# Moving columns taken alternately from the two halves of the operand, in the float32r matmuls of a spectral layer with two MLPs

## The chip, the cores and the metric

The kernel runs on one core of a Trainium2 chip. The metric is the device time in microseconds (us) of one execution. Engines: PE (TensorE) with its weight loads (PEld), DVE (VectorE), ACT (ScalarE), POOL (GpSimd), SP (the queue that issues most DMAs).

## The reference, cut to what matters

```
X = rfft(x, axis=1)                      # x: 2 x 3008 x 256, float32
Yr = Xr @ w_r - Xi @ w_i + b_r           # the mixing, 256 x 256
Yi = Xr @ w_i + Xi @ w_r + b_i
Y  = soft-threshold(Yr, 0.01) + 1j * soft-threshold(Yi, 0.01)
y  = irfft(Y, n=3008, axis=1)            # -> 6016 tokens x 256
h  = y @ w_in;  g = max(h, 0) + alpha * min(h, 0);  z = g @ w_out      # 256 -> 2048 -> 256
h  = z @ w_in2; g = where(h >= 1, h, where(h <= -1, 0, (h + 1)**2 / 4));  out = g @ w_out2
```

## The kernel before, in words

The transform of length 3008 = 47 x 64 is done in two stages. `f1` multiplies by a 47-point matrix (float32, 256 columns), stores its result to DRAM (`store_a`, halves 0 and 1 of the frequencies), and `load_a` brings it back in another layout. Then come 24 items (2 batches x 12), in the loop over `j`: `f2(j+2)` (the second forward matrices, tiles `m_t[0..2]`, eight frequencies each, so four items each), `mix(j)` (the mixing), `i1(j-2)` (the first inverse matrices, `n_t[0..2]`); `p3` is the second inverse stage and writes `y`. From item 16 on `p3` and the conversion of the first MLP's weights lie beside the items.

Where more than single-pass precision is wanted, an operand is split into a high and a low part of type float32r (`split`: the high part by ACT or DVE, the low part by DVE), and three matmuls are added up: low x high, high x low, high x high. `mm3` does this for the MLPs (L95 to L97), `mix` does it by itself (L324 to L326). In the MLPs the moving operand is the activation, 512 tokens (a chunk; the sixth chunk of each batch has 448), and the stationary operand is a block of 128 x 128 weights. In `mix` the moving operand is the weight `wm`, 256 columns, and the stationary one is the data. `f1`, `f2`, `i1` and `p3` use float32 operands without a split; each such matmul is two records in the trace.

An MLP step (layer l, chunk c, hidden block f) has two parts: `first` computes 128 hidden units of the chunk (6 matmuls into `psh`), the activation function and the split into `gh`, `gl`; `second`, three steps later, adds their share to the two output blocks `pso` (6 matmuls). After the last f the output is copied from `pso` to `y` (L439) and, in the second layer, stored. `prep` splits the next chunk's input into `mxh`, `mxl`. There are 2 x 12 x 16 = 384 steps. All tokens of a chunk are independent columns, so their order inside a chunk may be any, as long as the copy at the end puts them back.

The order on each engine is the program's order, written out by hand. So is that of SP's DMAs, which it issues one after the other; one that has to wait holds up all that follow:

```
    load_mn(0, n_t, c_i1)          # L282
    for g in range(8):
        store_a(g, 1)
    load_mn(1, m_t, c_f2)          # L285
    load_a(0, A_PARTS[3:])
    load_mn(2, m_t, c_f2)
    for g in range(8, 16):
        f1(g)
        store_a(g, 0)
    load_mn(1, n_t, c_i1)
```

Of the kernel before, what the change touches and what calls it, by code (L numbers as in the profile page):

```python
# [9 lines left out]
F32R = mybir.dt.float32r  # L10
U32 = mybir.dt.uint32
AF = mybir.ActivationFunctionType
# [9 lines left out]
NF = DFF // 128  # L22
# [53 lines left out]
def spectral_mlp_kernel(ctx: ExitStack, tc: tile.TileContext, x, w_r, w_i, bias, c_f1, c_f2,  # L76
                        c_i1, c_i2, w_in1, w_out1, alpha, w_in2, w_out2, out):
    nc = tc.nc
    V, A, G, T = nc.vector, nc.scalar, nc.gpsimd, nc.tensor

    base = ctx.enter_context(tc.tile_pool(name="base", bufs=1))
    rot = ctx.enter_context(tc.tile_pool(name="rot", bufs=2))
# [3 lines left out]
    def split(src, hi, lo, hi_engine):  # L86

        if hi_engine is A:
            A.activation(hi, src, AF.Copy)  # L89
        else:  # L90
            V.tensor_copy(hi, src)  # L91
        V.tensor_tensor(lo, src, hi.bitcast(F32), op=ALU.subtract)  # L92

    def mm3(ps, wh, wl, xh, xl, start, stop):
        T.matmul(ps, wl, xh, start=start, stop=False)  # L95
        T.matmul(ps, wh, xl, start=False, stop=False)  # L96
        T.matmul(ps, wh, xh, start=False, stop=stop)  # L97
# [5 lines left out]
    def block(tag, shape, dtype, name):  # L103
        return base.tile(shape, dtype, tag=tag, name=name)
# [22 lines left out]
    def w_of(l, k, f, h, sl):  # L127
        return wt[l, f][:, h, 256 * k + sl * 128:256 * k + sl * 128 + 128]
# [76 lines left out]
    ps = psum.tile([128, 256], F32, tag="h", name="ps_warm")  # L205
# [20 lines left out]
    def load_a(b, parts):  # L226
        if a_sb[b] is None:
            a_sb[b] = block(f"a{b}", [128, NK, D], F32, f"a_{b}")
        for k, n in parts:
            h, k0 = divmod(k, NK // 2)  # L230
            src = a_dr[b][h].rearrange("t (q k) f -> (t q) k f", q=4)
            nc.sync.dma_start(a_sb[b][:, k:k + n, :], src[:, k0:k0 + n, :])

    def store_a(g, h):
        b, j = divmod(g, 8)
        nc.sync.dma_start(a_dr[b][h][4 * j:4 * j + 4].rearrange("t p f -> p t f"), aes[g][48 * h:48 * h + 48])

    def load_mn(k, tiles, src):
        nc.sync.dma_start(tiles[k].rearrange("p k f -> p (k f)"), src[:, 1024 * k:1024 * (k + 1)])

    a_sb, aes = [None] * B, {}

# [21 lines left out]
    m_t = [block(f"m{k}", [128, 8, 128], F32, f"m{k}") for k in range(3)]  # L264
    n_t = [block(f"m{3 + k}", [128, 8, 128], F32, f"n{k}") for k in range(3)]
    wm32 = [rot.tile([128, 2, D], F32, tag="tb", name=f"wm32_{k}") for k in range(2)]
# [3 lines left out]
    for g in range(8):  # L270
        f1(g)
        store_a(g, 0)
        load_x(8 + g)
        if g == 3:
            nc.sync.dma_start(m_t[0][:, 0:4, :].rearrange("p k f -> p (k f)"), c_f2[:, 0:512])
    nc.sync.dma_start(wm32[0], w_r.rearrange("(c p) e -> p c e", p=128))
    load_a(0, A_PARTS[:2])
    nc.sync.dma_start(wm32[1], w_i.rearrange("(c p) e -> p c e", p=128))
    nc.sync.dma_start(m_t[0][:, 4:8, :].rearrange("p k f -> p (k f)"), c_f2[:, 512:1024])
    load_a(0, A_PARTS[2:3])  # L280
    nc.sync.dma_start(b_t[:, 0, :], bias)
    load_mn(0, n_t, c_i1)  # L282
    for g in range(8):
        store_a(g, 1)
    load_mn(1, m_t, c_f2)  # L285
    load_a(0, A_PARTS[3:])
    load_mn(2, m_t, c_f2)
    for g in range(8, 16):
        f1(g)
        store_a(g, 0)  # L290
    load_mn(1, n_t, c_i1)
    wm = [block(f"c{k}", [128, 2, 2, D], F32R, f"wm{k}") for k in range(2)]
    for k in range(2):
        split(wm32[k], wm[k][:, 0], wm[k][:, 1], A)


    items = [(b, i) for b in range(B) for i in range(NK // 2)]
# [17 lines left out]
    def mix(b, i):  # L315
        xh, xl = xt.pop((b, i))
        ps = psum.tile([128, 2, D], F32, tag="o", name=f"psm{b}_{i}")
        for k in range(2):
            o = ps[:, k, :]
            for c in range(2):  # L320
                j = 2 * k + c
                for r, off in ((0, 64), (1, 0)):
                    last = c == 1 and r == 1
                    T.matmul(o, xl[:, j, off:off + 128], wm[r][:, 0, c, :], start=c == r == 0, stop=False)  # L324
                    T.matmul(o, xh[:, j, off:off + 128], wm[r][:, 1, c, :], start=False, stop=False)  # L325
                    T.matmul(o, xh[:, j, off:off + 128], wm[r][:, 0, c, :], start=False, stop=last)  # L326
        cl_ = rot.tile([128, 2, D], F32, tag="ta", name=f"clip{b}_{i}")
        t = rot.tile([128, 2, D], F32, tag="tb", name=f"t{b}_{i}")
        y32 = rot.tile([128, 2, D], F32, tag="gh", bufs=4, name=f"y32_{b}_{i}")
        V.tensor_tensor(t, ps, b_t.to_broadcast([128, 2, D]), op=ALU.add)  # L330
        V.tensor_scalar(cl_, t, LAM, -LAM, op0=ALU.min, op1=ALU.max)
        V.tensor_tensor(y32, t, cl_, op=ALU.subtract)
        y_32[b, i] = y32
# [14 lines left out]
    chunks = []  # L348
    for b in range(B):
        c0 = 0  # L350
# [3 lines left out]
    NMAX = max(CHUNKS)  # L354
    NC = len(chunks)
    xc, gt, po = {}, {}, {}

    def window(n):

        return slice(0, n) if n == NMAX else slice(16, 16 + n)  # L360

    def prep(l, c):
        b, c0, n = chunks[c]

        tags = ("p1", "p2") if (l, c) == (0, 0) else (f"c{2 * (c % 2)}", f"c{2 * (c % 2) + 1}")
        xh, xl = (block(t, [128, 2, NMAX], F32R, f"mx{h}{l}_{c}")[:, :, window(n)] for t, h in zip(tags, "hl"))
        split(y[b][:, :, c0:c0 + n], xh, xl, A)
        xc[l, c] = xh, xl

    vs, y = {}, [None] * B  # L370

# [16 lines left out]
    def late_split(step):  # L388
        return step[0] == 1 or step[1] < 2 or step[1] == NC - 1

    def split_late(step):
        if step is not None and late_split(step):
            gh, gl, ta = gt[step]
            split(ta, gh, gl, A)

    def first(l, c, f, before):
        n = chunks[c][2]
        xh, xl = xc[l, c]
        ps = psum.tile([128, NMAX], F32, tag="h", name=f"psh{l}_{c}_{f}")[:, :n]
        for d in range(2):  # L400
            mm3(ps, w_of(l, 0, f, 0, d), w_of(l, 0, f, 1, d), xh[:, d, :], xl[:, d, :], d == 0, d == 1)
        gh = rot.tile([128, NMAX], F32R, tag="gh", bufs=4, name=f"gh{l}_{c}_{f}")[:, window(n)]
        gl = rot.tile([128, NMAX], F32R, tag="gl", bufs=4, name=f"gl{l}_{c}_{f}")[:, window(n)]
        ta = rot.tile([128, NMAX], F32, tag="ta", name=f"ta{l}_{c}_{f}")[:, :n]
        tb = rot.tile([128, NMAX], F32, tag="tb", name=f"tb{l}_{c}_{f}")[:, :n]
        gt[l, c, f] = gh, gl, ta
        if l == 0:

            A.activation(ta, ps, AF.Relu, scale=-1.0)  # L409
            A.activation(tb, ps, AF.Relu)  # L410
            split_late(before)
            V.scalar_tensor_tensor(ta, ta, nalpha[:, f:f + 1], tb, op0=ALU.mult, op1=ALU.add)  # L412
            if not late_split((l, c, f)):
                split(ta, gh, gl, V)
        else:

            A.activation(ta, ps, AF.Relu, bias=0.5, scale=0.5)  # L417
            V.scalar_tensor_tensor(tb, ta, 1.0, ta, op0=ALU.min, op1=ALU.mult)  # L418
            split_late(before)
            V.tensor_tensor(ta, ps, tb, op=ALU.max)  # L420

    def second(l, c, f):
        b, c0, n = chunks[c]
        gh, gl, _ = gt.pop((l, c, f))
        if f == 0:
            po[l, c] = [psum.tile([128, NMAX], F32, tag="o", name=f"pso{e}_{l}_{c}")[:, :n] for e in range(2)]
        for e in range(2):
            mm3(po[l, c][e], w_of(l, 1, f, 0, e), w_of(l, 1, f, 1, e), gh, gl, f == 0, f == NF - 1)
        if f == NF - 1:
            for e in range(2):  # L430
                dst = y[b][:, e, c0:c0 + n]
                if e and (l, c) == (1, NC - 1):
                    k = n // 2
                    V.tensor_copy(dst[:, :k], po[l, c][e][:, :k])
                    A.activation(dst[:, k:], po[l, c][e][:, k:], AF.Copy)
                    A.dma_start(out[:, e, b * S + c0 + k:b * S + c0 + n], dst[:, k:])
                    nc.sync.dma_start(out[:, e, b * S + c0:b * S + c0 + k], dst[:, :k])
                    continue
                A.activation(dst, po[l, c][e], AF.Copy)  # L439
                if l == 1:  # L440
                    nc.sync.dma_start(out[:, e, b * S + c0:b * S + c0 + n], dst)

    conv = conversions(0, list(range(NF)), V, V)
    n = len(items)
# [3 lines left out]
    for j in range(n):  # L448
        if j + 2 < n:
            f2(*items[j + 2])  # L450
        mix(*items[j])
        if j >= 2:
            i1(*items[j - 2])
# [22 lines left out]
        if j == n - 2:  # L476
            prep(0, 0)
# [13 lines left out]
    for i in range(len(seq) + DEPTH):  # L491
        if i < len(seq):
            l, c, f = seq[i]
# [57 lines left out]
```

## Time and profile before

| | us |
|---|---|
| median of 3 runs | 1208.13 (1204.58 to 1208.75) |
| the profiled execution, its own time | 1207.99 |
| its span | 1206.2 |
| PE busy / PEld / DVE / ACT / POOL | 1198.1 / 1025.4 / 905.7 / 607.4 / 80.4 |
| granted TensorE clock, mean | 0.999 |

A matmul's record begins before it streams and ends when its last result is modelled to be out, so two records that follow each other overlap; what a matmul costs is read from the distance between the starts of records, not from their length. Column order in the rows of a timeline: start in us, length in us, engine, line, operation, output <- inputs, shape, number of records merged, and in brackets the idle time before and what ended it.

### The profile page before, as it was taken

What the parts mean: (1) busy time and instruction counts of PE and PEld (TensorE: products, weight loads), DVE (VectorE), ACT (ScalarE), POOL (GpSimd) and SP (SyncE); (2) the same over time, 40 slices, a digit from 0 to 9 for tenths busy, and PEclk for the clock granted to TensorE, in tenths of its full rate; (3) what the DMA queues carried; (4) which work ended last, traced back from release to release, by engine and by line L of the source; (5) the groups of instructions that cost most, each with busy time, mean ns of one, the idle gap of its engine ahead of it and who ended that gap; (6) DMA issues with size and microseconds to landing.
All of it is one profiled execution on the core that took longest, in us unless ns stands there. A gap on an engine that the chain in (4) does not pass through costs nothing.

```text
span 1206.2 us, 15623 instructions
## 1 busy us (share of the span) xinstructions
PE 1198.1 (99%) x5862; PEld 1025.4 (85%) x5862; DVE 905.7 (75%) x1409; ACT 607.4 (50%) x1131; POOL 80.4 (7%) x64
## 2 busy tenths in 40 slices
PE   9999999999999999999999999999999999999998
PEld 6899988888888988888888988888889888888888
DVE  3489977368889999888875676777777777777775
ACT  3455676565555555554444644444444444444443
POOL 0000000001213131231200000000000000000000
PEclk9999999999999999999999999999999999999999
DMA  9995660010100101000000000000000000000000
GB/s 280 311 306 170 189 187 15 1 35 18 36 18 18 35 19 36 18 30 6 1 1 18 1 1 18 18 1 18 18 1 18 17 1 18 18 18 1 18 18 16
DMA packets 37180, 59.30 MB, mean 49 GB/s; under 512 B 3248, under 2 KB 25200, under 8 KB 37104
## 3 DMA queue, kind: packets, MB, share of 16 engines
q1 hardware_dynamic: 23536, 41.37, 10.7%
q10 hardware_dynamic: 13568, 16.93, 4.5%
q8 instruction: 46, 0.75, 0.3%
q14 instruction: 30, 0.25, 0.1%
HBM read 39.55 MB, written 18.74 MB: 48 GB/s over the span
## 4 chain that ended last, share of the span: by engine, by line
PE 96%; DMA 3%; SPq 1%; issue 0%; ACT 0%; DVE 0%
PE pso L97 14%; PE psh L97 14%; PE pso L96 14%; PE psh L96 14%; PE pso L95 14%; PE psh L95 14%; PE ps L383 2%; PE psm L324 2%; PE psm L325 2%; PE psm L326 2%; PE psi L339 2%; PE psf L304 2%; DMA x<-in_x 1%; DMA n<-in_c_i 1%; DMA a_dr<-ae 1%; DMA m<-in_c_f 0%
## 5 line engine op out<-in xcount | busy, mean ns | idle before, releaser
L92 DVE TENSOR_TENSOR gl<-ta,gh 128x512 fp32r<-128x512 f32 (+1 forms) x384 | 274.7, 715 | 60.8 <-ACT gh L89 55.8
L95 PE MATMUL pso<-gh,w 128*128 128x512 f32 (+1 forms) x768 | 296.0, 385 | 0.0
L95 PE MATMUL psh<-mxh,w 128*128 128x512 f32 (+1 forms) x768 | 295.8, 385 | 0.0
L96 PE MATMUL pso<-gl,w 128*128 128x512 f32 (+1 forms) x768 | 295.6, 385 | 0.0
L97 PE MATMUL pso<-gh,w 128*128 128x512 f32 (+1 forms) x768 | 295.5, 385 | 0.0
L96 PE MATMUL psh<-mxl,w 128*128 128x512 f32 (+1 forms) x768 | 295.5, 385 | 0.0
L97 PE MATMUL psh<-mxh,w 128*128 128x512 f32 (+1 forms) x768 | 295.5, 385 | 0.0
L417 ACT ACTIVATE ta<-psh 128x512 f32<-128x512 f32 (+1 forms) x192 | 113.1, 589 | 279.1 <-PE psh L97 279.1
L418 DVE SCALAR_TENSOR_TENSOR tb<-ta 128x512 f32<-128x512 f32 (+1 forms) x192 | 130.7, 681 | 143.4 <-ACT ta L417 143.4
L409 ACT ACTIVATE ta<-psh 128x512 f32<-128x512 f32 (+1 forms) x192 | 113.3, 590 | 235.2 <-PE psh L97 190.0
L412 DVE SCALAR_TENSOR_TENSOR ta<-ta,nalpha,tb 128x512 f32<-128x512 f32 (+1 forms) x192 | 166.9, 869 | 30.0 <-ACT tb L410 29.4
L96 PEld LDWEIGHTS psh<-mxl,w 128*128 128x128 f32 x768 | 144.2, 188 | 27.2
L96 PEld LDWEIGHTS pso<-gl,w 128*128 128x128 f32 x768 | 144.2, 188 | 26.9 <-DVE gl L92 0.2
L95 PEld LDWEIGHTS psh<-mxh,w 128*128 128x128 f32 x768 | 144.0, 188 | 27.0
L95 PEld LDWEIGHTS pso<-gh,w 128*128 128x128 f32 x768 | 144.1, 188 | 26.5
L97 PEld LDWEIGHTS psh<-mxh,w 128*128 128x128 f32 x768 | 144.2, 188 | 26.3
L97 PEld LDWEIGHTS pso<-gh,w 128*128 128x128 f32 x768 | 144.1, 188 | 26.2
L89 ACT ACTIVATE gh<-ta 128x512 fp32r<-128x512 f32 (+1 forms) x240 | 147.6, 615 | 1.3 <-DVE ta L420 1.3
L420 DVE TENSOR_TENSOR ta<-psh,tb 128x512 f32<-128x512 f32 (+1 forms) x192 | 129.2, 673 | 0.0
L410 ACT ACTIVATE tb<-psh 128x512 f32<-128x512 f32 (+1 forms) x192 | 112.3, 585 | 0.0
L91 DVE CAST gh<-ta 128x512 fp32r<-128x512 f32 (+1 forms) x144 | 68.1, 473 | 15.2 <-PE pso L97 0.5
L324 PE MATMUL psm<-wm,fl 128*128 128x256 f32 x192 | 56.3, 293 | 0.2 <-DVE fl L311 0.2
(56 smaller groups left out, 889.2 us busy)
## 6 DMA issues: line engine op xcount, KB each, us to landing
u<-in_w_in ACTq DMA_DIRECT2D x32, 256.0 KB, 2.7
u<-in_w_out ACTq DMA_DIRECT2D x32, 256.0 KB, 3.0
v_dr<-ve SPq DMA_DIRECT2D x12, 512.0 KB, 3.0
v<-v_dr SPq DMA_DIRECT2D x16, 384.0 KB, 5.1
x<-in_x SPq DMA_DIRECT2D x15, 384.0 KB, 7.5
out<-yt SPq DMA_DIRECT2D x20, 256.0 KB, 2.1
a<-a_dr SPq DMA_DIRECT2D x6, 768.0 KB, 7.5
a_dr<-ae SPq DMA_DIRECT2D x20, 192.0 KB, 7.0
```

The lines of the kernel that those rows point to most:

```text
L89: A.activation(hi, src, AF.Copy)
L92: V.tensor_tensor(lo, src, hi.bitcast(F32), op=ALU.subtract)
L95: T.matmul(ps, wl, xh, start=start, stop=False)
L96: T.matmul(ps, wh, xl, start=False, stop=False)
L97: T.matmul(ps, wh, xh, start=False, stop=stop)
L324: T.matmul(o, xl[:, j, off:off + 128], wm[r][:, 0, c, :], start=c == r == 0, stop=False)
L409: A.activation(ta, ps, AF.Relu, scale=-1.0)
L410: A.activation(tb, ps, AF.Relu)
L412: V.scalar_tensor_tensor(ta, ta, nalpha[:, f:f + 1], tb, op0=ALU.mult, op1=ALU.add)
L417: A.activation(ta, ps, AF.Relu, bias=0.5, scale=0.5)
L418: V.scalar_tensor_tensor(tb, ta, 1.0, ta, op0=ALU.min, op1=ALU.mult)
L420: V.tensor_tensor(ta, ps, tb, op=ALU.max)
```

## The change

Two things are changed. First, each float32r matmul of the MLPs and of the mixing gets its moving operand as pairs: column q of the first half, column q of the second half, then q + 1 of each. In a chunk of 512 the halves are 256 columns (1024 bytes) apart; a chunk of 448 is laid as two runs of 224 that begin 256 columns apart. The output is written in order, pair by pair, so the tokens in `psh` are in another order than in `mxh`; `second` does the same again, and the copy to `y` puts back the four quarters that have been interleaved. In `mix` the columns of `wm` are put into SBUF as two halves, so that the result is in its natural order. Second, the SP queue gets the first half of `m_t[1]` ahead of `n_t[0]` and ahead of the eight stores; `n_t[0]` comes in two halves, and `n_t[1]` ahead of `m_t[2]`.

```diff
-    def load_mn(k, tiles, src):
-        nc.sync.dma_start(tiles[k].rearrange("p k f -> p (k f)"), src[:, 1024 * k:1024 * (k + 1)])
+    def load_mn(k, tiles, src, h=None):
+        s = slice(0, 8) if h is None else slice(4 * h, 4 * h + 4)
+        nc.sync.dma_start(tiles[k][:, s, :].rearrange("p k f -> p (k f)"),
+                          src[:, 1024 * k + 128 * s.start:1024 * k + 128 * s.stop])
...
     load_a(0, A_PARTS[2:3])
     nc.sync.dma_start(b_t[:, 0, :], bias)
-    load_mn(0, n_t, c_i1)
+    load_mn(1, m_t, c_f2, 0)
+    load_mn(0, n_t, c_i1, 0)
     for g in range(8):
         store_a(g, 1)
-    load_mn(1, m_t, c_f2)
+    load_mn(1, m_t, c_f2, 1)
+    load_mn(0, n_t, c_i1, 1)
     load_a(0, A_PARTS[3:])
+    load_mn(1, n_t, c_i1)
     load_mn(2, m_t, c_f2)
     for g in range(8, 16):
         f1(g)
         store_a(g, 0)
-    load_mn(1, n_t, c_i1)
...
-        split(wm32[k], wm[k][:, 0], wm[k][:, 1], A)
+        hi, lo = (wm[k][:, z].rearrange("p c (h q) -> p c q h", h=2) for z in range(2))
+        split(wm32[k].rearrange("p c (q h) -> p c q h", h=2), hi, lo, A)
...
-            o = ps[:, k, :]
+            o = ps[:, k, :].rearrange("p (q h) -> p q h", h=2)
...
+                    wh, wl = (wm[r][:, z, c, :].rearrange("p (h q) -> p q h", h=2) for z in range(2))
+                    T.matmul(o, xl[:, j, off:off + 128], wh, start=c == r == 0, stop=False)
...
-    def window(n):
-        return slice(0, n) if n == NMAX else slice(16, 16 + n)
+    def halves(t, n):
+        return t if n == NMAX else t.rearrange("p (h q) -> p h q", h=2)[:, :, :n // 2]
+    def like_halves(t, n):
+        return t if n == NMAX else t.rearrange("p (h q) -> p h q", h=2)
+    def in_turn(t, n):
+        return t.rearrange("p (h q) -> p q h", h=2)[:, :n // 2, :]
+    def pairs(t):
+        return t.rearrange("p (q h) -> p q h", h=2)
+    def quarters(t):
+        return t.rearrange("p (q u v) -> p q u v", u=2, v=2)
+    def by_quarters(t):
+        return t.rearrange("p (u v q) -> p q u v", u=2, v=2)
...
+    def split_g(step, hi_engine):
+        n = chunks[step[1]][2]
+        gh, gl, ta = gt[step]
+        split(like_halves(ta, n), halves(gh, n), halves(gl, n), hi_engine)
...
-            mm3(ps, w_of(l, 0, f, 0, d), w_of(l, 0, f, 1, d), xh[:, d, :], xl[:, d, :], d == 0, d == 1)
+            mm3(pairs(ps), w_of(l, 0, f, 0, d), w_of(l, 0, f, 1, d), in_turn(xh[:, d, :], n), in_turn(xl[:, d, :], n),
+                d == 0, d == 1)
...
-            mm3(po[l, c][e], w_of(l, 1, f, 0, e), w_of(l, 1, f, 1, e), gh, gl, f == 0, f == NF - 1)
+            mm3(pairs(po[l, c][e]), w_of(l, 1, f, 0, e), w_of(l, 1, f, 1, e), in_turn(gh, n), in_turn(gl, n), f == 0,
+                f == NF - 1)
...
+                to, ps = by_quarters(dst), quarters(po[l, c][e])
...
-                A.activation(dst, po[l, c][e], AF.Copy)
+                A.activation(to, ps, AF.Copy)
```

## Rows read from the trace of the kernel before

**Rows 1.** The page: busy time (share of span) and instructions; chain that ended last.
```profile
PE 1198.1 (99%) x5862; PEld 1025.4 (85%) x5862; DVE 905.7 (75%) x1409; ACT 607.4 (50%) x1131; POOL 80.4 (7%) x64
PE 96%; DMA 3%; SPq 1%; issue 0%; ACT 0%; DVE 0%
```

**Rows 2.** Groups by line and form: busy us, mean ns, then idle before.
```profile
L95 PE MATMUL pso<-gh,w 128*128 128x512 f32 x640 | 249.8, 390 | 0.0
L95 PE MATMUL psh<-mxh,w 128*128 128x448 f32 x128 | 46.2, 361 | 0.0
L324 PE MATMUL psm<-wm,fl 128*128 128x256 f32 x192 | 56.3, 293 | 0.2 <-DVE fl L311 0.2
```

**Rows 3.** Timeline, first layer of 512 columns: a step's start and the next one's.
```profile
700.20 0.39 PE L95 MATMUL psh<-mxh,w 128*128 128x512 f32 x1
...
702.92 0.39 PE L95 MATMUL psh<-mxh,w 128*128 128x512 f32 x1
```

**Rows 4.** Timeline of PE, a chunk of 448 columns, twelve matmuls apart.
```profile
1169.94 0.36 PE L95 MATMUL psh<-mxh,w 128*128 128x448 f32 x1
...
1172.34 0.36 PE L95 MATMUL psh<-mxh,w 128*128 128x448 f32 x1
```

**Rows 5.** Timeline of PE in the items: mixing (22 matmuls apart), then float32 matmuls.
```profile
108.30 0.28 PE L325 MATMUL psm<-wm,fh 128*128 128x256 f32 x1
...
110.89 0.28 PE L326 MATMUL psm<-wm,fh 128*128 128x256 f32 x1
111.01 1.03 PE L339 MATMUL psi<-y,n 128*128 128x256 f32 x4
111.87 1.05 PE L304 MATMUL psf<-m,a 128*128 128x128 f32 x8
...
159.28 1.92 PE L383 MATMUL ps<-g,v 96*128 96x94 f32 x16
161.04 1.06 PE L339 MATMUL psi<-y,n 128*128 128x256 f32 x4
```

**Rows 6.** Timeline of PE around its longest wait, and the next undisturbed item.
```profile
43.57 0.28 PE L326 MATMUL psm<-wm,fh 128*128 128x256 f32 x1
46.07 1.99 PE L304 MATMUL psf<-m,a 128*128 128x128 f32 x8 [2.21 <-DMA m<-in_c_f]
...
51.44 1.02 PE L339 MATMUL psi<-y,n 128*128 128x256 f32 x4
52.30 1.05 PE L304 MATMUL psf<-m,a 128*128 128x128 f32 x8
...
56.02 1.03 PE L339 MATMUL psi<-y,n 128*128 128x256 f32 x4
```

**Rows 7.** Timeline of SP's DMA issues: start, issuing time, line, tiles, count.
```profile
32.53 0.45 SPq L239 DMA_DIRECT2D n<-in_c_i  x1
33.03 8.08 SPq L236 DMA_DIRECT2D a_dr<-ae  x8
41.15 0.56 SPq L239 DMA_DIRECT2D m<-in_c_f  x1
44.80 0.81 SPq L232 DMA_DIRECT2D a<-a_dr  x2
...
75.94 1.62 SPq L232 DMA_DIRECT2D a<-a_dr  x3
```

**Rows 8.** DMA issues from 75 to 79 us: KB, us to landing.
```profile
a<-a_dr SPq DMA_DIRECT2D x1, 512.0 KB, 6.6
a<-a_dr SPq DMA_DIRECT2D x1, 256.0 KB, 3.2
```

**Rows 9.** Busy time by stretch: PE, PEld, DVE, ACT, POOL, then clock and DMA.
```profile
40.00:60.00 20.00, 17.79 (x133) 17.40 (x132) 10.26 (x17) 6.92 (x16) 0.00 (x0) 0.91 0.93 315
70.00:100.00 30.00, 30.00 (x237) 29.29 (x236) 27.89 (x50) 17.55 (x37) 0.00 (x0) 1.00 0.77 259
440.00:480.00 40.00, 40.00 (x178) 33.11 (x177) 36.73 (x52) 19.98 (x37) 10.87 (x8) 1.00 0.09 28
700.00:800.00 100.00, 100.00 (x443) 82.81 (x442) 72.38 (x114) 46.05 (x81) 0.00 (x0) 1.00 0.03 11
```

**Rows 10.** Groups by line and form: copies with whole rows, and with every second word.
```profile
L439 ACT ACTIVATE yt<-pso 128x512 f32<-128x512 f32 x40 | 21.7, 602 | 0.0
L147 ACT ACTIVATE u<-u 128x512 f32<-128x512 uint32 x32 | 21.7, 677 | 0.0
```

More of the change, by code (lines that the diff above doesn't have):

```diff
@@ L274, in spectral_mlp_kernel @@
         if g == 3:
-            nc.sync.dma_start(m_t[0][:, 0:4, :].rearrange("p k f -> p (k f)"), c_f2[:, 0:512])
+            load_mn(0, m_t, c_f2, 0)
     nc.sync.dma_start(wm32[0], w_r.rearrange("(c p) e -> p c e", p=128))
@@ L278, in spectral_mlp_kernel @@
     nc.sync.dma_start(wm32[1], w_i.rearrange("(c p) e -> p c e", p=128))
-    nc.sync.dma_start(m_t[0][:, 4:8, :].rearrange("p k f -> p (k f)"), c_f2[:, 512:1024])
+    load_mn(0, m_t, c_f2, 1)
     load_a(0, A_PARTS[2:3])
     nc.sync.dma_start(b_t[:, 0, :], bias)
-    load_mn(0, n_t, c_i1)
+    load_mn(1, m_t, c_f2, 0)
+    load_mn(0, n_t, c_i1, 0)
     for g in range(8):
         store_a(g, 1)
-    load_mn(1, m_t, c_f2)
+    load_mn(1, m_t, c_f2, 1)
+    load_mn(0, n_t, c_i1, 1)
     load_a(0, A_PARTS[3:])
+    load_mn(1, n_t, c_i1)
     load_mn(2, m_t, c_f2)
@@ L323, in mix @@
                     last = c == 1 and r == 1
-                    T.matmul(o, xl[:, j, off:off + 128], wm[r][:, 0, c, :], start=c == r == 0, stop=False)
-                    T.matmul(o, xh[:, j, off:off + 128], wm[r][:, 1, c, :], start=False, stop=False)
-                    T.matmul(o, xh[:, j, off:off + 128], wm[r][:, 0, c, :], start=False, stop=last)
+                    wh, wl = (wm[r][:, z, c, :].rearrange("p (h q) -> p q h", h=2) for z in range(2))
+                    T.matmul(o, xl[:, j, off:off + 128], wh, start=c == r == 0, stop=False)
+                    T.matmul(o, xh[:, j, off:off + 128], wl, start=False, stop=False)
+                    T.matmul(o, xh[:, j, off:off + 128], wh, start=False, stop=last)
         cl_ = rot.tile([128, 2, D], F32, tag="ta", name=f"clip{b}_{i}")
@@ L365, in prep @@
         tags = ("p1", "p2") if (l, c) == (0, 0) else (f"c{2 * (c % 2)}", f"c{2 * (c % 2) + 1}")
-        xh, xl = (block(t, [128, 2, NMAX], F32R, f"mx{h}{l}_{c}")[:, :, window(n)] for t, h in zip(tags, "hl"))
-        split(y[b][:, :, c0:c0 + n], xh, xl, A)
+        xh, xl = (block(t, [128, 2, NMAX], F32R, f"mx{h}{l}_{c}") for t, h in zip(tags, "hl"))
         xc[l, c] = xh, xl
+        src = y[b][:, :, c0:c0 + n]
+        if n < NMAX:
+            src = src.rearrange("p d (h q) -> p d h q", h=2)
+            xh, xl = (t.rearrange("p d (h q) -> p d h q", h=2)[:, :, :, :n // 2] for t in (xh, xl))
+        split(src, xh, xl, A)
     vs, y = {}, [None] * B
@@ L392, in split_late @@
         if step is not None and late_split(step):
-            gh, gl, ta = gt[step]
-            split(ta, gh, gl, A)
+            split_g(step, A)
+    def split_g(step, hi_engine):
+        n = chunks[step[1]][2]
+        gh, gl, ta = gt[step]
+        split(like_halves(ta, n), halves(gh, n), halves(gl, n), hi_engine)
     def first(l, c, f, before):
@@ L400, in first @@
         for d in range(2):
-            mm3(ps, w_of(l, 0, f, 0, d), w_of(l, 0, f, 1, d), xh[:, d, :], xl[:, d, :], d == 0, d == 1)
-        gh = rot.tile([128, NMAX], F32R, tag="gh", bufs=4, name=f"gh{l}_{c}_{f}")[:, window(n)]
-        gl = rot.tile([128, NMAX], F32R, tag="gl", bufs=4, name=f"gl{l}_{c}_{f}")[:, window(n)]
+            mm3(pairs(ps), w_of(l, 0, f, 0, d), w_of(l, 0, f, 1, d), in_turn(xh[:, d, :], n), in_turn(xl[:, d, :], n),
+                d == 0, d == 1)
+        gh = rot.tile([128, NMAX], F32R, tag="gh", bufs=4, name=f"gh{l}_{c}_{f}")
+        gl = rot.tile([128, NMAX], F32R, tag="gl", bufs=4, name=f"gl{l}_{c}_{f}")
         ta = rot.tile([128, NMAX], F32, tag="ta", name=f"ta{l}_{c}_{f}")[:, :n]
@@ L413, in first @@
             if not late_split((l, c, f)):
-                split(ta, gh, gl, V)
+                split_g((l, c, f), V)
         else:
@@ L431, in second @@
                 dst = y[b][:, e, c0:c0 + n]
+                to, ps = by_quarters(dst), quarters(po[l, c][e])
                 if e and (l, c) == (1, NC - 1):
                     k = n // 2
-                    V.tensor_copy(dst[:, :k], po[l, c][e][:, :k])
-                    A.activation(dst[:, k:], po[l, c][e][:, k:], AF.Copy)
+                    V.tensor_copy(to[:, :, 0], ps[:, :, 0])
+                    A.activation(to[:, :, 1], ps[:, :, 1], AF.Copy)
                     A.dma_start(out[:, e, b * S + c0 + k:b * S + c0 + n], dst[:, k:])
```

## The prediction

> **What bounds the kernel now.** I read the page's busy times and its chain of waits first. PE is busy for 99% of the span and makes 96% of the chain [rows 1], so only what shortens PE's own sequence, or a wait inside it, moves the end. The groups by form say what fills PE: six lines of 640 matmuls with 512 columns (3840) and of 128 with 448 columns (768) in the MLPs, and three lines of 192 with 256 columns (576) in the mixing; one row of each stands in [rows 2], and the idle time before them is nil. Next comes their price. The records overlap, so I take distances between starts. A step of the MLP is twelve matmuls; from one step's first matmul to the next one's are 702.92 - 700.20 = 2.72 us, 226.7 ns each [rows 3]. At the granted clock of 1.00 [rows 9], 2.4 GHz, 512 columns at one per cycle would be 213.3 ns: 13.3 ns, 32 cycles, are over. At 448 columns it is 2.40 / 12 = 200.0 ns [rows 4] against 186.7: again 13.3. So this is a fixed price per matmul, not per column. In the mixing, 22 matmuls take 2.59 us, 117.7 ns each [rows 5], 11.0 over 106.7.
>
> Is it the change of weights? The float32 matmuls say no. Four records of `i1` take 111.87 - 111.01 = 0.86 us, 215 ns each [rows 5]; such a record streams 256 columns at two cycles each (213.3 ns), loads its own weights like the others, and has only 1.7 ns over. A stream that takes a column every second cycle shows hardly any gap; one that takes a column in every cycle shows 13.3 ns. I read this as a moving operand that is fetched just as fast as it is used: nothing is fetched ahead, so the start of the next operand is seen. This is an inference; no row shows the fetch.
>
> **The change part by part.** *Order of the moving columns.* Nothing is added to PE's list: the same 5184 float32r matmuls, the same columns. What changes is that every second column comes from the other half, so each half is walked through in sequence at one column per two cycles, as a float32 operand is. If the fetch can follow both halves side by side, each stream has the slack of the float32 one, and the gap should fall to near that one's. No row of before shows a moving operand read in such an order, so its price is bounded: from below by the columns alone, 213.3 ns; from above by a column per two cycles, 215 / 256 = 0.84 ns each, 430 ns for 512 [rows 5], and more than that can't be excluded. I take the float32 value and round it up to 216 ns, because that row has the same 512 cycles of streaming and the same weight loads. Then: 512 columns (226.7 - 216.0) x 3840 = 41.0 us; 448 columns (186.7 + 2.7 = 189.4), 10.6 x 768 = 8.2 us. In the mixing the weight load comes next: 16 records of `p3` stream only 94 columns twice over (78 ns) and still take 161.04 - 159.28 = 1.76 us, 110 ns each [rows 5]. So the mixing falls from 117.7 to 110 at best: 7.7 x 576 = 4.4 us.
>
> *Can the other engines follow?* A step would take 2.59 us where it took 2.72. The densest stretch for DVE has 36.73 us busy in 40 [rows 9], 92%; on PE's 38.1 us that is 96%. In the second layer it is 72% in 100 us. In the items DVE has 27.89 of 30 us; there PE gives back 24 x 7.7 ns = 0.18 us of an item's 4.58 (from [rows 6], 51.44 to 56.02), so DVE goes to 97%. It fits, but with little left; I charge nothing and keep a loss of some us in the range. `second` runs three steps after `first`, so the chain from `psh` to `gl` has over 7 us.
>
> *Copies that reorder.* The 48 copies of `pso` write to four places in turn. The nearest stepped row is the ACT copy that touches every second word, 677 ns against 602 [rows 10]; below, the step may cost nothing, above I allow four times 602. All but the last chunk's lie under PE, where ACT is busy for 46 us of 100 [rows 9]. In the tail I charge 0.1 us (at most 2). The four splits of `wm` write every column to the other half in turn: 0.2 us by the same ratio, ahead of the first mixing. The runs of 224 in the chunks of 448 I take as free.
>
> *The DMA order.* PE's longest wait is for `m_t[1]`: 2.21 us at 43.9 [rows 6]. The load was issued at 41.15, because SP had first to issue eight stores from 33.03 to 41.15 [rows 7]. The wait costs more than itself: after it the clock is down (0.91 over 40 to 60 us [rows 9]), and the eight `f2` records take 1.99 us instead of 1.05. From the last mixing matmul to the next `i1` are 51.44 - 43.57 = 7.87 us; undisturbed it is 0.12 + 56.02 - 52.30 = 3.84. So 4.0 us go if the first half, issued at about 32.6, is there 11 us later. What SP issues ahead of and behind the eight stores has the same bytes as before up to the `load_a` at 44.80, since the halves of `m_t[1]` and `n_t[0]` only change places; `n_t[1]` then goes ahead of `m_t[2]`, which is wanted two items later.
>
> *What is late next.* With PE about 5.5 us ahead at item 12 (4.0, and 0.18 for each of some 9 items), the second batch's `load_a` is the next thing to come late: issued from 75.94 on [rows 7], its first 256 KB land 3.2 us later, at 79.1, and the next 512 KB 6.6 us after an issue at about 76.4, at 83.0 [rows 8]. Item 12's `f2`, seven items of 4.58 us after the one at 52.30 [rows 6], began at 84.4; it would now be wanted at 78.9, and item 13's at 83.3. A wait of some tenths of a us is possible, more if its clock falls too. I charge 0.5 us, from nil to 3.5.
>
> *Sum,* against the profiled execution's 1208.0 us (span 1206.2), which is 0.1 below the median shown: 41.0 + 8.2 + 4.4 + 4.0 = 57.6 less 0.1 + 0.2 + 0.5 = 0.8 gives 56.8; **1151 us**.
>
> **The rivals.** *Slower: switching between two places costs a cycle.* If the fetch works on one piece of the operand at a time, two neighbours that are 1024 bytes apart make it go back and forth for every column. For it speaks that the present stream, with neighbours side by side, already shows a gap, so it has no slack to spend; against it, that the distance between the matmuls is steady over hundreds of them, that is, nothing is lost inside a matmul now. At a column per two cycles: 512 columns 430 - 226.7 = 203 ns x 3840 = 781 us, 448 columns 376 - 200 = 176 x 768 = 135, mixing 215 - 117.7 = 97 x 576 = 56; with the front's 3 us off, about 2177 us. It decides from small amounts on: at more than 32 extra cycles in 512 columns, one stall in 16 columns, the change loses.
> [...]
>
> *The order makes no difference.* If the 13.3 ns belong to the float32r mode itself (how weights are taken over in it, say), only the front's 4.0 less 0.8 us remain: 1205 us. For it: the gap is the same 32 cycles at 512 and 448 columns, whatever tiles are read. Against: the mixing's gap is 11.0, so it isn't quite a constant.
>
> *Half of it.* The gap shrinks but doesn't vanish, or DVE, at 96%, holds PE up between 240 and 600 us: half of 53.6 and the front, 26.8 + 3.2 = 30, 1178 us.
>
> **How the numbers follow.** Forecast 0.53; half 0.15; no difference 0.12; slower 0.20. Anything within 0.5%, 6 us, is about what a measurement can't tell from no change; so faster 0.68, same 0.12, slower 0.20. The range goes from 1140 (columns without any gap: 13.3 x 4608 = 61 us, with 4.4 and 3.2) to 1212 (no difference and a few us lost to DVE or waits), which leaves out the slower case. The forecast's own range is 1140 to 1162.
>
> **What would show it.** In the profile after: step to step 2.59 us at 512 columns (2.72 if the order is nothing, about 5 if the stream halves); 189 ns at 448; 110 to 112 in the mixing; no wait for `m_t[1]` near 44 us and a clock of 1.00 from 40 to 60 us; a new short wait for `a` near 79 us; DVE at 95% or more between 320 and 520 us. If steps are short but PE idles between them, the loss is DVE's; if PE's matmuls are longer than 227 ns, the reading of the gap was wrong.

## The result, and the profile after

The changed kernel takes 1153.2 us (median of four runs, 1152.09 to 1154.64); the kernel before took 1206.7 in the same sessions (1204.58 to 1208.75). The ratio is 0.9557 with a 95% interval of 0.9535 to 0.958, so it is faster by 53.5 us. The forecast was 1151. The profiled execution took 1153.21 us, its span 1151.4; before, 1208.0 and 1206.2. The page's busy times and its chain of waits, in the order of [rows 1]: PE is the bound as before, but 5% of the chain now lies with DVE and ACT, nearly all of it from 160 to 182 us and from 386 to 417 us, both beside the conversion of weights.

```profile
PE 1143.5 (99%) x5862; PEld 1026.3 (89%) x5862; DVE 905.6 (79%) x1409; ACT 631.4 (55%) x1131; POOL 81.7 (7%) x64
...
PE 93%; DVE 3%; DMA 2%; ACT 2%; issue 1%; SPq 0%; ACTq 0%; DVEq 0%
```

PE runs the same 5862 matmuls as before; so look at the distance from one start to the next. Timeline of PE (start, duration, engine, line, tiles) in the second layer: the first matmul of one step of 512 columns and of the next, twelve matmuls on.

```profile
700.17 0.38 PE L95 MATMUL psh<-mxh,w 128*128 128x512 f32 x1
...
702.76 0.38 PE L95 MATMUL psh<-mxh,w 128*128 128x512 f32 x1
...
1143.10 0.35 PE L95 MATMUL pso<-gh,w 128*128 128x448 f32 x1
...
1145.37 0.35 PE L95 MATMUL pso<-gh,w 128*128 128x448 f32 x1
```

2.59 us for twelve, 215.8 ns each, where [rows 3] had 226.7; at 448 columns 2.27 us, 189.2 ns each, for 200.0 in [rows 4]. Of the 13.3 ns over the columns 2.5 are left. In the mixing, 19 matmuls of 256 columns are 2.12 us apart, 111.6 ns each, for 117.7 in [rows 5]:

```profile
100.05 0.28 PE L333 MATMUL psm<-wm,fh 128*128 128x256 f32 x1
...
102.17 0.28 PE L334 MATMUL psm<-wm,fh 128*128 128x256 f32 x1
```

The same view at the two places of the front where the DMA order should show (a bracket gives the idle time before a record and who ended it):

```profile
43.60 0.28 PE L334 MATMUL psm<-wm,fh 128*128 128x256 f32 x1
43.72 1.06 PE L311 MATMUL psf<-m,a 128*128 128x128 f32 x8
...
47.29 1.03 PE L347 MATMUL psi<-y,n 128*128 128x256 f32 x4
...
78.34 1.03 PE L347 MATMUL psi<-y,n 128*128 128x256 f32 x4
...
80.86 1.16 PE L311 MATMUL psf<-m,a 128*128 128x128 f32 x8 [1.49 <-DMA a<-a_dr]
```

The wait for `m_t[1]` of [rows 6] is gone: `f2` starts 0.12 us after the last mixing matmul, and `i1` 3.69 us after that matmul where it took 7.87. At item 12 there is a new wait of 1.49 us for `a`. Its cause is in SP's issues (start, time to issue, line):

```profile
33.67 8.00 SPq L236 DMA_DIRECT2D a_dr<-ae  x8
...
42.91 0.35 SPq L241 DMA_DIRECT2D m<-in_c_f  x1
...
45.09 6.28 SPq L232 DMA_DIRECT2D a<-a_dr  x2
...
75.88 2.08 SPq L232 DMA_DIRECT2D a<-a_dr  x3
```

The two `a` loads behind the stores hold SP for 6.28 us where they took 0.81 [rows 7], and the second batch's three go out at 75.88, no earlier than before (75.94) while PE is earlier by more than 3 us.

Busy time by stretch (PE, PEld, DVE, ACT, POOL, then granted clock, DMA share, GB/s), the stretches of [rows 9]:

```profile
40.00:60.00 20.00, 20.00 (x170) 19.69 (x170) 13.64 (x23) 9.57 (x22) 0.00 (x0) 1.00 0.89 296
...
440.00:480.00 40.00, 40.00 (x187) 35.04 (x186) 37.94 (x54) 23.22 (x40) 10.99 (x8) 1.00 0.07 22
```

PE makes 170 records where it made 133 from 40 to 60 us, at a clock of 1.00 instead of 0.91, and 187 for 178 from 440 to 480 us. DVE is 95% busy in the second of these stretches (93 to 95% over all of 320 to 520 us, 96% from 100 to 130 us in the items). Between 320 and 520 us DVE holds PE in one place, where the chain's stretch from 386 to 417 us ends: in a chunk of 448 columns, from 413.8 to 417.1 us, four distances are 251 to 438 ns instead of 189, 0.5 us in all. One of them:

```profile
416.36 0.35 PE L95 MATMUL pso<-gh,w 128*128 128x448 f32 x1
416.80 0.46 PE L96 MATMUL pso<-gl,w 128*128 128x448 f32 x1
```

The groups of copies and of stepped operations (count | busy us, mean ns | idle before):

```profile
L476 ACT ACTIVATE yt<-pso 128x512 f32<-128x512 f32 x40 | 40.4, 1125 | 0.0
...
L147 ACT ACTIVATE u<-u 128x512 f32<-128x512 uint32 x32 | 27.0, 844 | 0.0
L148 DVE TENSOR_SCALAR cp<-u 128x512 uint32<-128x512 uint32 x32 | 15.7, 490 | 0.0
```

The copies of `pso` went from 602 [rows 10] to 1125 ns. L147, which the diff doesn't touch, went from 677 to 844, and L148 from 421 to 490. The copies lie under PE, all but the last chunk's. L147 doesn't quite: between 160 and 182 us the chain of waits runs through it to PE (start, length, what):

```profile
179.79 0.96 ACT u L147
...
181.20 0.50 ACT tb L445
...
181.74 0.48 PE psh L95
```

Summed over all of PE's records as distances from start to start, in us:

| matmuls | before | after | difference |
|---|---|---|---|
| MLP, 512 columns | 872.5 | 830.6 | -41.9 |
| MLP, 448 columns | 153.7 | 146.0 | -7.7 |
| mixing | 73.2 | 66.4 | -6.8 (3.5 rate, 3.3 the wait for `m_t[1]` and the low clock after it) |
| `f2` | 21.7 | 20.9 | -0.8 |
| `i1` | 20.4 | 22.1 | +1.7 (the wait for `a`) |
| `f1` | 29.3 | 29.7 | +0.4 |
| first to last start | 1201.1 | 1146.0 | -55.1 |
| last start to the span's end | 4.0 | 4.2 | +0.3 |

### The profile page after: what moved, and what is told of

Its sections match the earlier page's. It is cut to its first block, busy times and chain, and to the rows that moved or that the text cites. A ratio compares the mean times of both kernels' runs of the same rounds, so it can differ in the third digit from the quotient of the medians.

```text
span 1151.4 us, 15803 instructions
## 1 busy us (share of the span) xinstructions
PE 1143.5 (99%) x5862; PEld 1026.3 (89%) x5862; DVE 905.6 (79%) x1409; ACT 631.4 (55%) x1131; POOL 81.7 (7%) x64
## 3 DMA queue, kind: packets, MB, share of 16 engines
q1 hardware_dynamic: 23824, 41.37, 11.3%
## 4 chain that ended last, share of the span: by engine, by line
PE 93%; DVE 3%; DMA 2%; ACT 2%; issue 1%; SPq 0%; ACTq 0%; DVEq 0%
PE pso L96 13%; PE pso L97 13%; PE pso L95 13%; PE psh L95 13%; PE psh L97 13%; PE psh L96 13%; PE ps L413 2%; PE ps L258 2%; PE psm L332 2%; PE psf L311 2%; PE psm L334 2%; PE psm L333 2%; PE psi L347 2%; DVE ta L447 1%; DVE gl L92 1%; DMA x<-in_x 1%
## 5 line engine op out<-in xcount | busy, mean ns | idle before, releaser
L95 PE MATMUL pso<-gh,w 128*128 128x512 f32 (+1 forms) x768 | 288.3, 375 | 0.0
L96 PE MATMUL pso<-gl,w 128*128 128x512 f32 (+1 forms) x768 | 288.2, 375 | 0.1
L95 PE MATMUL psh<-mxh,w 128*128 128x512 f32 (+1 forms) x768 | 288.2, 375 | 0.1
L96 PE MATMUL psh<-mxl,w 128*128 128x512 f32 (+1 forms) x768 | 287.8, 375 | 0.0
L97 PE MATMUL pso<-gh,w 128*128 128x512 f32 (+1 forms) x768 | 287.7, 375 | 0.0
L97 PE MATMUL psh<-mxh,w 128*128 128x512 f32 (+1 forms) x768 | 287.7, 375 | 0.0
```

## Experiments

Three questions were open: why the gap shrinks, what the DMA order is worth, and what the dearer copies cost. The edits are shown in their main lines; they are against the changed kernel except for the one called DMA order alone.

**Which order closes the gap.** One kernel whose MLP takes the columns in another order in each chunk. A chunk's order is the same for both operands, and results come out in permuted columns.

```diff
+def moving(t, l, c, n):              # kind k and distance d chosen by chunk
...
+    if k == "d":                     # pairs d columns apart
+        return t.rearrange("p (b h q) -> p b q h", h=2, q=d)
+    if k == "w":                     # two from each half at a time
+        return t.rearrange("p (h q v) -> p q h v", h=2, v=2)
+    if k == "s":                     # every d-th column
+        return t.rearrange("p (q s) -> p s q", s=d)
+    if k == "hs":                    # both halves in turn, each in steps of d
+        return t.rearrange("p (h q s) -> p s q h", h=2, s=d)
```

> The changed kernel, but the order in which an MLP matmul takes its 512 moving columns is another one in each chunk; the output columns stay in sequence, so tokens end up permuted inside a chunk. Read: start-to-start distance of the matmuls of each chunk. Orders: natural; pairs (q, q + D) inside blocks of 2 D for D = 1 (the natural sequence, written as pairs), 2, 4, 8, 16, 32, 64, 128, 256; two from each half at a time (A0 A1 B0 B1); every second, fourth, eighth column; alternate halves, but each half walked in steps of four columns. Theory 1 (even and odd places of the order are fetched as two streams, and a stream has slack when it takes four neighbouring columns, 16 bytes, in a row): natural and D = 1 226.7 ns, D = 2 226.7, D = 4 and all above 216; two from each half at a time, steps of two, four and eight, and stepped halves clearly above 227, up to 430 or more, because there each stream goes to another 16 bytes with every column. Theory 2 (what helps is that neighbours in the order lie far apart): D = 2, 4 and 8 stay at 227, only far pairs and all stepped orders fall to 216. Theory 3 (only the fact that the pattern has an inner run of two counts): D = 1 gives 216 too.

Measured in one execution, with a granted clock of 1.00 in all these chunks: mean ns from start to start over a chunk's 512-column matmuls (155 records each). "Even places" are the first, third, fifth column taken, and so on; the third column says how many of these in a row lie in one aligned run of four columns. The odd places go the same way.

| order | ns | even places in a row in one run of four |
|---|---|---|
| natural | 226.7 | 2 |
| pairs 2 apart | 226.7 | 2 |
| pairs 4, 8, 16, 32, 64, 128 or 256 apart | 215.8 | 4 |
| two from each half at a time | 339.9 | 1, but back to the run once |
| every 2nd, 4th, 8th column | 453, 461, 431 | 1 |
| halves in turn, each in steps of four | 453 | 1 |

Timeline of PE in that kernel, six matmuls apart in each pair of rows: pairs 2 apart, pairs 4 apart, steps of four, two from each half, steps of two.

```profile
320.55 0.39 PE L95 MATMUL psh<-mxh,w 128*128 128x512 f32 x1
...
321.91 0.39 PE L95 MATMUL pso<-gh,w 128*128 128x512 f32 x1
...
370.25 0.38 PE L95 MATMUL pso<-gh,w 128*128 128x512 f32 x1
...
371.55 0.38 PE L95 MATMUL psh<-mxh,w 128*128 128x512 f32 x1
...
576.85 0.64 PE L95 MATMUL pso<-gh,w 128*128 128x512 f32 x1
...
579.62 0.64 PE L95 MATMUL psh<-mxh,w 128*128 128x512 f32 x1
...
1101.13 0.51 PE L95 MATMUL psh<-mxh,w 128*128 128x512 f32 x1
...
1103.17 0.51 PE L95 MATMUL pso<-gh,w 128*128 128x512 f32 x1
...
1162.96 0.63 PE L95 MATMUL pso<-gh,w 128*128 128x512 f32 x1
...
1165.68 0.63 PE L95 MATMUL psh<-mxh,w 128*128 128x512 f32 x1
```

1.36, 1.30, 2.77, 2.04 and 2.72 us for six. Two halves aren't needed, nor distance: pairs 4 columns apart do as well as pairs 256 apart (215.8 ns both), and pairs 2 apart do nothing (226.7). Nor is it which columns are taken close together: two from each half at a time takes the same eight columns as two halves in turn do, and needs 339.9 ns for 215.8. What sorts all fourteen orders is the run of four, counted for even and odd places apart. With four in a row the gap is gone but for 2.5 ns, with two it is 13.3 ns, with one the matmul takes about twice its time, 431 to 461 ns (339.9 where it comes back to the run). That the chip fetches even and odd places as two streams is a reading that fits; the table shows the counts, not the fetch. Pairs 1 apart are the natural order and so no test of their own.

**The column order alone,** with the DMA order of before.

```diff
-    load_mn(1, m_t, c_f2, 0)
-    load_mn(0, n_t, c_i1, 0)
+    load_mn(0, n_t, c_i1)
...
-    load_mn(1, m_t, c_f2, 1)
-    load_mn(0, n_t, c_i1, 1)
+    load_mn(1, m_t, c_f2)
     load_a(0, A_PARTS[3:])
-    load_mn(1, n_t, c_i1)
...
+    load_mn(1, n_t, c_i1)
```

> Only the order of the moving columns is changed; DMAs as before. My theory: MLP and mixing as in the changed kernel (216, 189, 112 ns), the wait for m_t[1] near 44 us and the low clock after it are back (4.0 us), the wait for a near 79 us is gone (1.7 us): 1153.2 + 4.0 - 1.7 = 1155.5 us. Rival: the DMA order is worth several us more or less than that through the queue, below 1153 or above 1159.

Measured 1152.8 us (1152.16 to 1153.05), ratio 0.9559, 0.9544 to 0.9573: the whole gain of the change, as the rival had it and not the 1155.5 that was looked for. Its waits of PE (us in total, times, longest):

```profile
PE psf L306 <- DMA m<-in_c_f: 1.5, 1, 1.5
```

Timeline of SP's issues of `a` there:

```profile
43.92 0.81 SPq L232 DMA_DIRECT2D a<-a_dr  x2
...
72.83 1.90 SPq L232 DMA_DIRECT2D a<-a_dr  x3
```

PE waits for `m_t[1]`, 1.5 us, but the clock stays at 1.00 from 40 to 60 us. SP isn't held at 43.92, sends the second batch's loads at 72.83, three us earlier than after the full change, and PE doesn't wait for `a`. So the DMA order trades one wait for another of the same size.

**The DMA order alone,** on the kernel before: the reverse of that diff.

> Only the DMA order is changed; columns as before. My theory: PE's wait for m_t[1] and the clock dip go (4.0 us), and item 12 now waits some tenths of a us for a: 1206.7 - 3.6 = 1203 us. Rival: the whole gain comes back as waits further on, 1206.7.

Measured 1204.5 us (1202.45 to 1205.91), ratio 0.999, 0.998 to 0.9999: 1.2 us (nearly nil to 2.4), not 4. SP's issues of `a`, by the timeline:

```profile
43.49 7.08 SPq L232 DMA_DIRECT2D a<-a_dr  x2
...
75.99 1.72 SPq L232 DMA_DIRECT2D a<-a_dr  x3
```

PE's wait for them:

```profile
PE psf L309 <- DMA a<-a_dr: 1.2, 1, 1.2
```

The hold of SP and the wait for `a` come with the DMA order, without any change of columns; 0.7 us of waiting for `m` are left as well. The two profiled executions are 3.7 us apart (spans 1202.5 and 1206.2), three times the difference of the medians: the one of before, at 1208.0 us, lies 1.3 us above its own median.

**Second batch's loads earlier.** The first two parts are issued before an `n_t` load, not behind it.

```diff
+            load_a(1, A_PARTS[:2])
             load_mn(2, n_t, c_i1)
...
-            load_a(1, A_PARTS[:3])
+            load_a(1, A_PARTS[2:3])
```

> The changed kernel, with the first two loads of the second batch's a issued right behind the last stores, ahead of n_t[2], alpha and the second inverse matrix. My theory: item 12's wait of 1.65 us near 79 us goes, 1153.2 - 1.7 = 1151.5 us. Rival: SP is held by the stores' landing, the loads are issued hardly earlier and the wait stays, 1153.2; or n_t[2] becomes late for the i1 of item 8, above 1153.

Measured 1155.7 us (1154.74 to 1156.37), ratio 0.9583, 0.9569 to 0.9597: no gain. It is 2.5 us above the 1153.2 of the change, but 1.1 above the 1154.6 that the change took when it ran again (below), and the intervals overlap; that it is slower isn't established. Timeline of SP, the first two of the loads:

```profile
74.62 0.81 SPq L232 DMA_DIRECT2D a<-a_dr  x2
```

Timeline of ACT and PE after it:

```profile
83.48 0.60 ACT L350 ACTIVATE ve<-psi 128x512 f32<-128x512 f32 x1 [7.47 <-DMA v_dr<-ve]
84.13 1.13 PE L347 MATMUL psi<-y,n 128*128 128x256 f32 x4 [1.26 <-ACT ve L350]
```

The loads go 1.3 us earlier, but the store of `v` queues behind them; `ve` isn't free, ACT waits 7.47 us and PE 1.26. The wait moved, it didn't go.

**Where the hold comes from: `n_t[1]` moved back.** The next edit takes back the halves as well.

```diff
-    load_mn(1, n_t, c_i1)
     ...                              # the stores
+    load_mn(1, n_t, c_i1)
```

> The changed kernel with n_t[1] put back to its old place behind the stores of f1. Theory 1 (what item 12 waits for near 79 us is late because n_t[1]'s 512 KB were put ahead of the second batch's stores): load_a of the second batch is issued about 1.5 us earlier than at 75.9 us and the wait of 1.65 us goes, 1151.5 us. Theory 2 (it is late because two loads were cut in halves, which fills the queue with twice as many descriptors, so that SP is held at the load_a near 45 us for 6 us): the hold stays, and so does the wait, 1153.

Measured 1156.5 us (1155.18 to 1157.93), ratio 0.9593, 0.9579 to 0.9606. SP's issue, by the timeline:

```profile
45.02 7.49 SPq L232 DMA_DIRECT2D a<-a_dr  x2
```

PE's longest wait:

```profile
PE psi L347 <- DMA n<-in_c_i: 3.6, 1, 3.6
```

The hold stays, so it isn't `n_t[1]`'s doing. `n_t[1]`, now further behind the held loads, is late by 3.6 us, a part of `m` by 1.9, and the clock is 0.91 from 60 to 80 us. That these loads would be late wasn't foreseen. With PE itself that late the wait for `a` doesn't show, though `a` goes out later still, at 77.1 us.

**`m_t[1]` whole ahead of the stores, `n_t[0]` whole behind them.**

```diff
-    load_mn(1, m_t, c_f2, 0)
-    load_mn(0, n_t, c_i1, 0)
+    load_mn(1, m_t, c_f2)
...
-    load_mn(1, m_t, c_f2, 1)
-    load_mn(0, n_t, c_i1, 1)
+    load_mn(0, n_t, c_i1)
     load_a(0, A_PARTS[3:])
-    load_mn(1, n_t, c_i1)
...
+    load_mn(1, n_t, c_i1)
```

> The changed kernel with m_t[1] loaded whole ahead of the eight stores and n_t[0] whole behind them, n_t[1] at its old place: as many DMAs as before the change. Theory 2: SP is not held at load_a near 45 us, load_a of the second batch is issued near 73 us as in the run with only the column order, and both waits (m_t[1] and a) are gone: 1152.8 - 1.8 = 1151 us. Theory 1 gives the same here. Rival: n_t[0], now issued near 41 us, is late for the first i1 at 47.3 us, and the time is 1153 or more.

Measured 1153.4 us (1152.7 to 1155.6), ratio 0.957, 0.9557 to 0.9583. SP's issues:

```profile
44.50 0.81 SPq L232 DMA_DIRECT2D a<-a_dr  x2
...
74.35 3.63 SPq L232 DMA_DIRECT2D a<-a_dr  x3
```

Without halves the hold is gone, and no wait of PE at these places is over 0.7 us. Still the time isn't lower. In all runs whose loads are halved SP is held for 6.3 to 8.7 us near 45 us, and in those without halves for 0.8 to 1.2. The pages show 288 packets more on that queue with the two loads halved (23824 for 23536); why that holds SP isn't shown. That the time doesn't follow may in part be noise of the front: `f1`, which waits for the `x` loads, is 1.7 us over its undisturbed time (216 ns a record) in the profiled run of before and 2.0 after, and the first two loads of `a`, which SP issues ahead of everything that these edits touch, went out at 28.05 us with the column order alone, at 28.77 after the change and at 30.03 when the change ran again: up to 2 us, as much as these edits are worth.

**Copies without the four places.** The output's columns are then out of order.

```diff
-                to, ps = by_quarters(dst), quarters(po[l, c][e])
+                to, ps = quarters(dst), quarters(po[l, c][e])
```

> The changed kernel, but the 48 copies of pso leave the tokens in the order in which they stand (contiguous copies; the output's tokens are permuted inside each chunk). My theory: a copy takes 602 ns again where it takes 1125, but all but the last two lie under PE, so the time falls by the tail's 0.3 us alone, 1153 us. Rival: ACT, held 1 us longer at each chunk's end, delays the next steps, and the time falls by 1 to 3 us.

Measured 1154.5 us (1152.67 to 1154.77), ratio 0.9573, 0.956 to 0.9586: no gain. The group of copies:

```profile
L476 ACT ACTIVATE yt<-pso 128x512 f32<-128x512 f32 x40 | 21.7, 602 | 0.0
```

The price falls from 1125 to 602 ns, the time doesn't: 40 x 0.52 = 21 us of ACT lie under PE.

**Pairs 32 apart instead of 256,** in the MLP. The result, the copies to `y` and the chunks of 448 are laid out to match (not shown).

```diff
-        return t.rearrange("p (h q) -> p q h", h=2)[:, :n // 2, :]
+        return t[:, :n].rearrange("p (b h q) -> p b q h", h=2, q=32)
```

> The changed kernel with pairs (q, q + 32) inside blocks of 64 columns instead of the chunk's halves in the MLPs; the copies put blocks of 64 back in order; chunks of 448 lie contiguous. Theory 1 (a stream needs four neighbouring columns in a row, the distance of the two is free): 216 and 189 ns as with halves. From the table of orders: ACT and DVE operations that step over every second word, slowed to 880 to 930 ns beside pairs 1024 bytes apart, go back to 670 to 700 ns. Time the same or up to 1.5 us less, 1152.5 us, since only the stretch from 156 to 185 us has waits for ACT and DVE.

Measured 1152.2 us (1151.52 to 1154.54), ratio 0.9559, 0.9546 to 0.9572; 216 and 189 ns per matmul, as after. The group:

```profile
L147 ACT ACTIVATE u<-u 128x512 f32<-128x512 uint32 x32 | 23.1, 721 | 0.0
```

L147 falls from 844 to 721 ns, and 0.5 us that PE lost between 166 and 182 us are gone; the median is 1 us lower, which is within the noise. The layout in halves for 448 columns isn't needed.

**All that helped together:** whole `m_t[1]`, pairs 32 apart in the MLP, and blocks of 64 for `wm` in the mixing.

```diff
-    load_mn(1, m_t, c_f2, 0)
+    load_mn(1, m_t, c_f2)
...
-        return t.rearrange("p (h q) -> p q h", h=2)[:, :n // 2, :]
+        return t[:, :n].rearrange("p (b h q) -> p b q h", h=2, q=32)
...
-                    wh, wl = (wm[r][:, z, c, :].rearrange("p (h q) -> p q h", h=2) for z in range(2))
+                    wh, wl = (wm[r][:, z, c, :].rearrange("p (b h q) -> p b q h", h=2, q=32) for z in range(2))
```

> Pairs 32 columns apart in the MLPs and in the mixing, and m_t[1] loaded whole ahead of the stores, n_t[0] behind them. My theory: 216, 189 and 112 ns as in the changed kernel, no wait over 1 us for m_t[1] or a, ACT operations that step over every second word at 670 to 720 ns also in the items; 1151.5 us against the changed kernel's 1153.2 on the same chip, a gain of 0.1 to 0.2%. Rival: the first 80 us are set by DMA anyway, what one wait gives another takes, and both are equal within 0.1%.

Beside it, on the same chip, the changed kernel again, with no edit:

> The changed kernel itself, as the measure for the combined one on the same chip: 1153.2 us, the wait of some 1.7 us for a near 79 us again.

Measured: combined 1152.0 us (1151.53 to 1154.43), ratio 0.9555, 0.9538 to 0.9572; the changed kernel 1154.6 (1153.77 to 1157.49), ratio 0.9574, 0.9556 to 0.9593. The medians are 0.2% apart and the ranges overlap; that the combined kernel is faster isn't established. Longest wait of PE for a load, first the combined kernel, then the change run again:

```profile
PE psi L345 <- DMA n<-in_c_i: 1.5, 1, 1.5
PE psf L311 <- DMA a<-a_dr: 3.8, 2, 3.3
```

The combined kernel has no wait over 0.2 us for `m` and none for `a`, as expected, but now one for `n_t`, of 1.5 us. In the change's profiled execution, its slowest (1157.49 us), the wait for `a` is 3.8 us, not 1.5, and the clock is 0.91 from 80 to 100 us: this wait isn't the same from one execution to the next. The combined kernel's L147 takes 694 ns, nearly the 677 of before [rows 10]:

```profile
L147 ACT ACTIVATE u<-u 128x512 f32<-128x512 uint32 x32 | 22.2, 694 | 0.0
```

## Why the prediction was right

**The bound and the gap.** The step that carried the forecast holds: PE's sequence sets the end, the price over the columns is fixed per matmul (13.3 ns at 512 and at 448 columns), and it falls to near that of the float32 matmuls, 2.5 ns for 1.7, when every second column comes from the other half. The price of a column itself, 213.3 / 512 = 0.417 ns in the forecast, is what the two lengths show: 226.7 - 200.0 = 26.7 ns for 64 columns [rows 3, 4], and 215.8 - 189.2 = 26.6 after; a float32 record takes twice that, 215 ns for 256 columns [rows 5]. 216.0 was forecast, 215.8 measured: 41.9 us for 41.0. At 448 columns 189.2 for 189.4, and 7.7 us for 8.2; the 0.5 us at 414 us are what is missing. The order table makes the cause firmer than the forecast had it: what counts isn't that there are two halves, but that every second column taken stays in one run of four (215.8 ns with pairs 4 to 256 apart). So the forecast's picture of the gap, one stream that has no slack, is only half right: pairs 2 apart also alternate between two places, each walked at half the rate, and gain nothing (226.7 ns).

**The mixing** gave 6.1 ns a matmul, not 7.7; 3.5 us for 4.4. A floor was named; it is 111.6, not 110. The 110 was misread by a little: of sixteen `p3` records the first distance is 85 ns and the others are 111.5 on average. The loads of weights run without a break beside these `p3` records, 16 of them in 1.97 us from 159.07 us on PEld; that they set the floor was the author's reading and isn't shown.

**The slower rival** needed a stall when two neighbours lie far apart. Pairs 1024 bytes apart cost nothing (215.8 ns); two from each half at a time does cost: 339.9 ns, which would have made this a loss of (339.9 - 226.7) x 3840 = 435 us at 512 columns alone. So there is such a stall, but in the table it goes by whether each second column stays in its run of four, and not by how far apart two neighbours are. Two in a row in one run aren't quite enough here: they leave 13.3 ns a matmul, and four leave 2.5.

**No difference** is out: the 13.3 ns don't belong to the mode, since the order changes them. **Half of it** is out too: DVE came to 93 to 95% from 320 to 520 us, where 95% or more was forecast, and held PE for 0.5 us.

**The DMA order** is the term that was mis-sized: 4.0 less 0.5 for the wait for `a`, 3.5 in all. By the two traces 3.3 + 0.8 = 4.1 us are gained around `m_t[1]`, as forecast, and 1.7 lost at `a`, for 0.5. By the runs even that is too much: alone it gives 1.2 us, on top of the column order nothing that can be seen (1153.2 with it, 1152.8 without). Two steps failed. The fall of the clock, 4.0 - 2.2 = 1.8 us, was taken as belonging to the wait, yet with a wait of 1.5 us the clock stayed at 1.00 in the kernel with the column order alone. Nor does the length of a wait settle it: the clock fell, to 0.91 on average over 20 us, after waits of 2.2 us (before), 3.3 (the change run again) and 3.6 (`n_t[1]` moved back), but stayed at 1.00 around one of 3.2 in the order table's kernel. And the forecast took SP's issues behind the stores as unchanged, because the bytes are; SP was held 6 to 8 us there. The wait for `a`, 1.5 us, was in its bounds (nil to 3.5) in one execution and at 3.8 us just out of them in another. The loads' time of issue, 75.9, was the forecast's, but it goes with SP's hold: 75.9 to 77.7 in the kernels that have the hold and these loads in their old place, 72.8 to 74.4 in the three with the new columns and no hold.

**The copies** were priced at 677/602 of their old time, and take 1125/602; the splits of `wm` go from 624 and 685 to about 1137 ns. The forecast's argument, that they lie under PE, is what held; the tail grew by 0.3 us, 0.1 forecast. That L147 and L148 would slow down, and L147 hold PE for 0.5 us, was in no term.

**The sum.** Forecast -56.8 us; in the spans -54.8. The columns' terms missed by +0.9 - 0.5 - 0.9 = -0.5, and the rest is the front. That 1151 came within some 2 us of 1153.2 is in part luck: the forecast starts from an execution 1.3 us above its median and takes off 3.3 us more than the medians differ by (53.5), and the one slip takes back a part of the other.

## What to carry to other kernels

Compare the distance from start to start with the price of the columns alone (here 0.417 ns each, by the difference between 512 and 448 columns) before looking at idle time: here 11 ns over it per matmul, on an engine 99% busy, were worth 4%. For float32r operands lay out the moving columns so that every second one taken stays in one run of four; pairs 4 columns apart are enough (215.8 ns here for 226.7), and short distances disturb other engines less (`L147` at 0.69 us beside pairs 32 apart, 0.91 beside pairs 256 apart). A wait that one profiled run shows, with a fall of the clock or without, needn't be worth its length in that run: take the edit alone and time it.

## What the runs showed that was not expected

Operations of ACT and DVE that touch every second word got slower though nothing in them changed (`L147` from 677 to 844 ns, `L148` from 421 to 490), and in the MLPs, of the four orders shown here, only beside pairs 1024 bytes apart. In the order table's kernel, timeline of ACT, L147 beside the natural order, pairs 4, 32 and 256 apart:

```profile
266.53 0.69 ACT L147 ACTIVATE u<-u 128x512 f32<-128x512 uint32 x1
...
353.73 0.68 ACT L147 ACTIVATE u<-u 128x512 f32<-128x512 uint32 x1
...
432.65 0.69 ACT L147 ACTIVATE u<-u 128x512 f32<-128x512 uint32 x1
...
473.71 0.91 ACT L147 ACTIVATE u<-u 128x512 f32<-128x512 uint32 x1
```

0.68 to 0.69 us up to 128 bytes, 0.91 at 1024. In the items, beside the mixing's pairs, single ones take up to 0.84 us at 512 bytes (up to 0.69 before the change); in the combined kernel, with pairs 128 bytes apart everywhere, the mean of all 32 is 694 ns. So PE's order of reading reaches other engines; by what way isn't shown. Against the kernel with pairs 32 apart, PE loses some 0.5 us by it here, between 166 and 182 us; what it costs a kernel bound by ACT or DVE wasn't measured.
